# Threshold attention followed by a tanh-shrink layer, one core: one threshold shift for two tiles, earlier weights, DMA transposes from the second batch on, an earlier first projection and a last tile in halves

## The chip, the cores and the metric

One core of one Trainium2 chip. The time is the device time of one execution in microseconds (us). Stages are told from the profile of one execution; its span (first to last instruction) is some 2 us shorter than the device time.

## The reference, cut to what matters

```python
# q, k, v: (batch 8, heads 8, seq 576, head_dim 64), float32; tau = 0.02
scores = scale * q @ k.T
thresh = max(scores, axis=-1) - tau
scores = where(scores >= thresh, scores, -1e9)
attn   = softmax(scores)                      # over the surviving keys
x      = (attn @ v), heads side by side       # (4608, 512)
h = x @ w_in                                  # 512 -> 2048
g = h - tanh(h)
out = g @ w_out                               # 2048 -> 512
```

## The kernel before

Attention runs over 32 head pairs (four for each of eight batches), nine score tiles a pair: per head four whole tiles, which make two "duos" of an A and a B tile, and one M tile that both heads share. So 36 tiles are one batch. While batch m's attention runs, the hidden layer of batch m-1 and the projection of batch m-2 are slipped in as "layer steps" of four matmuls each. A last block holds the 64 remaining rows of every batch.

Names that the profile uses: `sc` the scaled scores with their row maximum `mx`; `nb` = tau - max, the shift; `z` = Prelu(sc + nb) with an enormous negative slope, so that a key below the threshold goes to a large negative number (`zm` where it is an M tile's); `zT` (or `psZ`, where TensorE does it) its transpose; `pT` = exp of it; `psO`, `osb`, `xT` the attention output on its way to the layers; `psH`, `th`, `g` the hidden layer; `psY`, `yo` the projection; `khl`, `qhl` the split of k and q on GpSimd, `kT`, `qT` their transposes, `kS` is kT with its two halves of 64 partitions exchanged; `wt` a piece of weights as loaded, `w_in_sb` and `w_out_sb` the cast weights.

Score and shift, per tile (VectorE):

```python
        mx = st_pool.tile([P, 1], F32, name="mx", tag="mx")
        nc.vector.tensor_scalar(
            out=sc, in0=ps[:, lo : lo + S], scalar1=SC, scalar2=None,
            op0=ALU.mult, op1=ALU.max, accum_out=mx,
        )
...
    def shift(i):
        sc, mx = scs[i]
        nb = st_pool.tile([P, 1], F32, name="nb", tag="nb")
        nc.vector.tensor_scalar(
            out=nb, in0=mx, scalar1=-1.0, scalar2=tau, op0=ALU.mult, op1=ALU.add
        )
```

The transpose of z, on TensorE for the first two batches (`NPE = 2 * HPAIR * TPP` tiles) and by DMA from batch 2 on:

```python
        if i < NPE:
            z = zts.pop(i)
            ps = ps_y.tile([P, 5 * P], BF16, name="psZ", tag="y")   # ps_y has one buffer
            for c in range(n):
                nc.tensor.matmul(..., rhs=ident_bf, is_transpose=True, ...)
            ...nc.scalar.activation(out=pt[...], in_=ps[:, 0 : n * P], func=ACT.Exp)
        # else: one exp over both tiles of the duo, from zT,
        # which kink() had made with nc.sync.dma_start_transpose(...)
```

kS and the weights (all of these DMAs are issued on the SyncE queue):

```python
            sw = qk_pool.tile([P, W], FP16, name="kS", tag="ks")
            nc.gpsimd.tensor_copy(out=sw[0:D, :], in_=m[D:P, :])
            nc.gpsimd.tensor_copy(out=sw[D:P, :], in_=m[0:D, :])
...
    wt_pool = pool("wt", 2)
    w_when = [4 * i + 3 for i in range(17)]
...
            if s + AHEAD in w_when:        # once per spacing: cast one, load the next
                if loaded:
                    w_cast()               # GpSimd
                piece = next(pieces, None)
                if piece:
                    w_load(piece)          # nc.sync.dma_start
```

`AHEAD = 7` and `MASK = 5` are leads in tiles: scores stand seven tiles, z five tiles ahead of the exp of the same tile.

Of the kernel before, what the change touches and what calls it, by code (L numbers as in the profile page):

```python
# [18 lines left out]
def kernel(  # L19
# [11 lines left out]
    nc = tc.nc  # L31
# [22 lines left out]
    NPE = 2 * HPAIR * TPP  # L54
# [4 lines left out]
    MASK = 5  # L59
# [21 lines left out]
    for i in range(NV):  # L81
        vb = const.tile([P, 2, 6, D + 1], BF16, name=f"vb{i}")
        nc.gpsimd.memset(vb[:, :, 4:6, :], 0.0)
        nc.vector.memset(vb[:, :, 0:4, D : D + 1], 1.0)
        nc.vector.memset(vb[0:64, :, 4, D : D + 1], 1.0)
        nc.vector.memset(vb[64:P, :, 5, D : D + 1], 1.0)
        vbs.append(vb)
# [3 lines left out]
    for i in range(NM):  # L91
# [9 lines left out]
    fold = const.tile([P, 64], BF16, name="fold")  # L101
    nc.vector.tensor_tensor(
        out=fold, in0=ident_bf[:, 0:64], in1=ident_bf[:, 64:P], op=ALU.add
    )

# [119 lines left out]
    def turn(p, t):  # L225
        hl = hls.pop((p, t))
        ps = ps_big.tile([P, W], FP16, name=f"ps_{t}", tag="big")
        for c in range(TPP):
            turn_chunk(
                ps[:, c * P : (c + 1) * P], c, hl[:, c, :, :].rearrange("p a d -> p (a d)")  # L230
            )
        m = qk_pool.tile([P, W], FP16, name=f"{t}T", tag=t)
        nc.vector.tensor_copy(out=m, in_=ps)  # L233
        mats[p, t] = m
        if t == "k":
            sw = qk_pool.tile([P, W], FP16, name="kS", tag="ks")
            nc.gpsimd.tensor_copy(out=sw[0:D, :], in_=m[D:P, :])  # L237
            nc.gpsimd.tensor_copy(out=sw[D:P, :], in_=m[0:D, :])  # L238
            mats[p, "ks"] = sw
# [25 lines left out]
    scs, zs, zts, pts, ops = {}, {}, {}, {}, {}  # L265
# [5 lines left out]
    def scores(i):  # L271
# [15 lines left out]
        else:  # L287
# [9 lines left out]
        mx = st_pool.tile([P, 1], F32, name="mx", tag="mx")  # L297
        nc.vector.tensor_scalar(  # L298
            out=sc, in0=ps[:, lo : lo + S], scalar1=SC, scalar2=None,
            op0=ALU.mult, op1=ALU.max, accum_out=mx,  # L300
        )
        scs[i] = sc, mx

    def shift(i):
        sc, mx = scs[i]
        nb = st_pool.tile([P, 1], F32, name="nb", tag="nb")
        nc.vector.tensor_scalar(  # L307
            out=nb, in0=mx, scalar1=-1.0, scalar2=tau, op0=ALU.mult, op1=ALU.add
        )
        scs[i] = sc, nb  # L310

    def kink(i):
        sc, nb = scs.pop(i)
# [20 lines left out]
    def weights(i):  # L334
# [4 lines left out]
        if i < NPE:  # L339
            z = zts.pop(i)  # L340
            ps = ps_y.tile([P, 5 * P], BF16, name="psZ", tag="y")
# [126 lines left out]
    def project(m, ms, part, ps, last):  # L468
        for n in range(4 * part, 4 * part + 4):
            nc.tensor.matmul(  # L470
                out=ps, lhsT=gs[m][:, n, ms * P : (ms + 1) * P],
                rhs=w_out_sb[:, n, :], start=(n == 0), stop=(n == DF_C - 1),
            )
        if part == 3:
            yo = y_pool.tile([P, d_model], F32, name="yo")
# [7 lines left out]
            else:  # L483
                for h in range(2):
                    b = 2 * ms + h
                    stores.append(
                        lambda b=b, h=h: nc.sync.dma_start(
                            out=out[b * S + MB : (b + 1) * S, :],
# [3 lines left out]

    def layers(m, tail):

        steps, cur = [], {}
# [8 lines left out]
        def y_step(ms, part):  # L504
            if part == 0:
                tag = ("y", "o")[ms % 2] if tail else "y"
                pl = {"y": ps_y, "o": ps_o}[tag]
                cur["y"] = pl.tile([P, d_model], F32, name="psY", tag=tag)
            project(m - 1, ms, part, cur["y"], tail and ms % 2)

        for a in range(16):
            if m < NMB:
                steps.append(lambda a=a: h_step(a))
            if m > 0:
                steps.append(lambda a=a: y_step(a // 4, a % 4))
        return steps

# [49 lines left out]
    for t in ("k", "q", "ks"):  # L567
        turn_first(t, 0)
    split_v(0)
# [3 lines left out]
    w_when = [4 * i + 3 for i in range(17)]  # L573
# [59 lines left out]
    while stage <= NMB:  # L633
# [45 lines left out]
```

## Time and profile before

| | before |
|---|---|
| device time, median of 4 runs | 551.97 us (551.58 to 552.21) |
| span of the profiled run | 549.4 us |
| TensorE / VectorE / ScalarE / GpSimd busy | 95 / 81 / 81 / 52 % |
| start and batch 0 (to the copy of its last pair's x) | 71.14 us |
| batch 1 | 58.25 us |
| batches 2 to 6 (59.16 or 59.17 each) | 295.82 us |
| batch 7 (no hidden layer of its own yet) | 50.86 us |
| tail, layers alone | 73.3 us |

The stage lengths are read from the trace: every fourth head pair's x copy closes a batch. The lines on which they rest stand in the prediction below. There and later, a line of waits says who waited, for whom, and then us in all, times and the longest; a line of the timeline gives start, length, engine, line and instruction, and in brackets the idle time before it and what ended that; L307 is line 307 of that run's own kernel, so the same instruction has another number in another kernel.

### The profile page before, as it was taken

Reading aid. Unit: us, or ns where it says so; the run is one execution under the profiler, and the core shown is the slowest. Engines: PE = TensorE matmul, PEld = TensorE weight load, DVE = VectorE, ACT = ScalarE, POOL = GpSimd, SP = SyncE. Lnnn points to the kernel's source line nnn. Section 1 sums busy time; section 2 is a strip of 40 time slices with the busy share of each in tenths; the row PEclk is TensorE's granted clock in tenths of the full one; section 3 lists DMA queues with packets and bytes.
Section 4 is the critical chain, followed back from the end, with each engine's and each line's share of the span. In section 5 each row is a group of like instructions: output and inputs, shape, how many; then the busy total and the mean of one; then the engine's idle time right before and its main releaser. Section 6 shows DMA issues by size and latency. Waiting matters only on the chain.

```text
span 549.4 us, 13518 instructions
## 1 busy us (share of the span) xinstructions
PE 521.8 (95%) x4954; PEld 302.4 (55%) x4954; DVE 444.1 (81%) x1349; ACT 443.3 (81%) x640; POOL 286.5 (52%) x372
## 2 busy tenths in 40 slices
PE   5888999999999999999999999999999999999996
PEld 2566666665555555555555555555555555444442
DVE  5888988898988999898889898898989888544430
ACT  3999999899899898989888988989898989533320
POOL 6788977666556666556555655666665620000000
PEclk9999999999999999999999999999999999999999
DMA  6755644437879888889977798877878966310103
GB/s 168 216 183 146 205 125 145 128 74 157 161 153 172 178 181 160 169 171 170 186 174 173 165 182 164 167 180 179 163 169 171 185 87 144 66 39 38 40 38 78
DMA packets 183011, 80.33 MB, mean 146 GB/s; under 512 B 150688, under 2 KB 175264, under 8 KB 182944
## 3 DMA queue, kind: packets, MB, share of 16 engines
q1 hardware_dynamic: 182512, 79.17, 65.0%
q8 instruction: 39, 0.64, 0.5%
q10 hardware_dynamic: 432, 0.30, 0.2%
q14 instruction: 28, 0.23, 0.2%
HBM read 37.75 MB, written 9.44 MB: 86 GB/s over the span
## 4 chain that ended last, share of the span: by engine, by line
PE 72%; DVE 16%; ACT 8%; issue 2%; DMA 1%; SPq 0%; ACTq 0%; DVEq 0%
PE psY L470 20%; PE psH L444 18%; PE psS L292 15%; DVE sc L298 6%; PE psO L389 5%; ACT pT L352 4%; PE psS L282 3%; ACT z L324 3%; DVE g L463 3%; PE psHt L444 3%; PE ps_q L221 2%; PE ps_k L221 2%; PE psZ L343 2%; DVE yo L479 1%; DVE kT L233 1%
## 5 line engine op out<-in xcount | busy, mean ns | idle before, releaser
L298 DVE TENSOR_SCALAR_CACHE_REDUCE sc<-psS 128x576 f32<-128x576 f32 x288 | 216.3, 751 | 19.8 <-PE psS L282 12.5
L324 ACT ACTIVATE z<-sc,nb 128x576 bf16<-128x576 f32 x256 | 195.7, 769 | 14.3 <-DVE nb L307 13.4
L470 PE MATMUL psY<-w_out_sb,g 128*128 128x512 bf16 x576 | 145.4, 379 | 0.0
L360 ACT ACTIVATE pT<-zT 128x1152 f16<-128x1152 bf16 (+1 forms) x120 | 127.8, 1065 | 0.0
L444 PE MATMUL psH<-xT,w_in_sb 128*128 128x512 bf16 x480 | 124.0, 379 | 0.3
L292 PE MATMUL psS<-kT,qT 128*128 128x512 f16 (+1 forms) x512 | 105.2, 287 | 10.1 <-DVE nb L307 7.6
L292 PEld LDWEIGHTS <-qT 128*128 128x128 f16 x1024 | 75.5, 98 | 68.1 <-issue 15.9
L237 POOL COPY kS<-kT 64x1152 f16<-64x1152 f16 x31 | 35.3, 1140 | 141.4 <-DVE nb L307 141.4
L463 DVE SCALAR_TENSOR_TENSOR g<-th,psH 128x512 bf16<-128x512 f32 x128 | 87.4, 683 | 22.0 <-ACT th L457 22.0
L292 PE MATMUL psS<-kS,qT 128*128 128x512 f16 x496 | 101.4, 286 | 0.0
L457 ACT ACTIVATE th<-psH 128x512 f32<-128x512 f32 x128 | 74.7, 584 | 17.8 <-PE psH L444 17.6
L470 PEld LDWEIGHTS <-g 128*128 128x128 bf16 x576 | 49.6, 98 | 57.7 <-issue 2.6
L444 PEld LDWEIGHTS <-w_in_sb 128*128 128x128 bf16 x576 | 49.3, 98 | 55.0 <-issue 2.7
L389 PEld LDWEIGHTS <-pT 128*128 128x128 f16 x1280 | 55.6, 98 | 24.3 <-ACT pT L360 2.1
L389 PE MATMUL psO<-vb,pT 128*128 128x65 bf16 x1280 | 61.2, 193 | 0.6 <-ACT pT L360 0.6
L352 ACT ACTIVATE pT<-psZ 128x640 f16<-128x640 bf16 (+1 forms) x72 | 47.2, 656 | 6.9 <-PE psZ L343 6.2
L307 DVE TENSOR_SCALAR nb<-mx 128x1 f32<-128x1 f32 x288 | 42.6, 148 | 3.4
L324 ACT ACTIVATE zm<-sc,nb 128x576 bf16<-128x576 f32 x32 | 24.8, 774 | 23.1 <-DVE nb L307 23.1
L183 POOL TENSOR_TENSOR qhl<-xs,qhl 128x576 f16<-128x576 f32 x31 | 39.7, 1280 | 2.6
L183 POOL TENSOR_TENSOR khl<-xs,khl 128x576 f16<-128x576 f32 x31 | 39.7, 1279 | 2.6
L238 POOL COPY kS<-kT 64x1152 f16<-64x1152 f16 x31 | 35.4, 1142 | 1.3
L343 PE MATMUL psZ<-ident_bf,z 128*128 128x128 bf16 x288 | 26.5, 219 | 4.5 <-ACT pT L352 4.3
(72 smaller groups left out, 561.6 us busy)
## 6 DMA issues: line engine op xcount, KB each, us to landing
vraw<-in_v_dram SPq DMA_DIRECT2D x32, 256.0 KB, 3.5
out_dram<-yo SPq DMA_DIRECT2D x32, 256.0 KB, 2.6
kraw<-in_k_dram SPq DMA_DIRECT2D x31, 256.0 KB, 3.1
qraw<-in_q_dram SPq DMA_DIRECT2D x31, 256.0 KB, 3.2
wt<-in_moe_w_in_dram SPq DMA_DIRECT2D x8, 512.0 KB, 4.4
wt<-in_moe_w_out_dram SPq DMA_DIRECT2D x8, 512.0 KB, 3.9
vraw<-in_v_dram SPq DMA_DIRECT2D x64, 32.0 KB, 2.9
zT<-z SPq DMA_TRANSPOSE x96, 3.3
```

The lines of the kernel that those rows point to most:

```text
L183: nc.gpsimd.tensor_tensor(out=hl[:, :, 1, :], in0=x, in1=hl[:, :, 0, :], op=ALU.subtract)
L292: nc.tensor.matmul(out=ps[:, dst], lhsT=lhs, rhs=kk[:, src], start=(n == 0), stop=(n == 1),)
L298: nc.vector.tensor_scalar(out=sc, in0=ps[:, lo : lo + S], scalar1=SC, scalar2=None, op0=ALU.mult, op1=ALU.max, accum_out=mx,)
L307: nc.vector.tensor_scalar(out=nb, in0=mx, scalar1=-1.0, scalar2=tau, op0=ALU.mult, op1=ALU.add)
L324: nc.scalar.activation(out=z, in_=sc, func=ACT.Prelu, bias=nb, scale=1.0, alpha=STEEP)
L352: nc.scalar.activation(out=pt[:, off * P : (off + n) * P], in_=ps[:, 0 : n * P], func=ACT.Exp)
L360: nc.scalar.activation(out=pt[:, 0 : n * P], in_=zts.pop(i)[:, 0:n, :], func=ACT.Exp)
L389: nc.tensor.matmul(out=po[:, (j - 1 - 5 * hh) + ab, :], lhsT=pt[:, blk * P : (blk + 1) * P], rhs=vb[:, hh, c, :], start=(n == 0), stop=(n ...
L444: nc.tensor.matmul(out=ps, lhsT=w_in_sb[:, c, n * P : (n + 1) * P], rhs=xs[m][:, c, :] if m < B else xR[:, c, :, :], start=(c == 0), stop= ...
L457: nc.scalar.activation(out=th, in_=ps, func=ACT.Tanh)
L463: nc.vector.scalar_tensor_tensor(out=gs[m][:, n, :], in0=th, scalar=-1.0, in1=ps, op0=ALU.mult, op1=ALU.add,)
L470: nc.tensor.matmul(out=ps, lhsT=gs[m][:, n, ms * P : (ms + 1) * P], rhs=w_out_sb[:, n, :], start=(n == 0), stop=(n == DF_C - 1),)
```

## The change

The intent is to take work off the engines at their limit. One shift serves both tiles of a duo; the lead of z falls from five tiles to four, so that both maxima of a duo exist in time. The DMA transposes (called the "crossbar" in places below) take over from batch 1 on instead of batch 2, counting from 0, and the batch that stays with TensorE alternates between two PSUM pools. kS comes by DMA for batch 0, weights come every three tiles instead of four, three projection steps move a stage earlier, and the last tile of the output is made and stored in halves.

```diff
-    NPE = 2 * HPAIR * TPP
+    NPE = HPAIR * TPP
-    MASK = 5
+    MASK = 4
...
-            nc.gpsimd.tensor_copy(out=sw[0:D, :], in_=m[D:P, :])
-            nc.gpsimd.tensor_copy(out=sw[D:P, :], in_=m[0:D, :])
+            for lo, hi in ((0, D), (D, 0)):
+                o, i = sw[lo : lo + D, :], m[hi : hi + D, :]
+                if p < HPAIR:
+                    nc.sync.dma_start(out=o, in_=i)
+                else:
+                    nc.gpsimd.tensor_copy(out=o, in_=i)
...
-        mx = st_pool.tile([P, 1], F32, name="mx", tag="mx")
+        if kind(j) == "B":
+            mx = mxs[i] = mxs.pop(i - 1)
+        else:
+            mx = mxs[i] = st_pool.tile([P, 2], F32, name="mx", tag="mx")
...
     def shift(i):
+        kd = kind(i % TPP)
+        if kd == "A":
+            return
+        n = 2 if kd == "B" else 1
+        nb = st_pool.tile([P, 2], F32, name="nb", tag="nb")
         nc.vector.tensor_scalar(
-            out=nb, in0=mx, scalar1=-1.0, scalar2=tau, op0=ALU.mult, op1=ALU.add
+            out=nb[:, 0:n], in0=mx[:, 0:n], scalar1=-1.0, scalar2=tau,
+            op0=ALU.mult, op1=ALU.add,
         )
...
-            ps = ps_y.tile([P, 5 * P], BF16, name="psZ", tag="y")
+            pl, tag = ((ps_y, "y"), (ps_h, "h"))[i % 2]
+            ps = pl.tile([P, 5 * P], BF16, name="psZ", tag=tag)
...
+    EARLY = 3        # projection steps of a block done in its own stage
+    # layers(): order of steps rebuilt for this; the last tile as two
+    # halves of 256 columns, one copied by ScalarE and stored on its queue
...
-    w_when = [4 * i + 3 for i in range(17)]
+    w_when = [3 * i + 2 for i in range(17)]
```

Left out: constants moved from VectorE to GpSimd or to later, and the bookkeeping of the layer steps.

More of the change, by code (lines that the diff above doesn't have):

```diff
@@ L83 @@
         nc.gpsimd.memset(vb[:, :, 4:6, :], 0.0)
-        nc.vector.memset(vb[:, :, 0:4, D : D + 1], 1.0)
-        nc.vector.memset(vb[0:64, :, 4, D : D + 1], 1.0)
-        nc.vector.memset(vb[64:P, :, 5, D : D + 1], 1.0)
+        nc.gpsimd.memset(vb[:, :, 0:4, D : D + 1], 1.0)
+        nc.gpsimd.memset(vb[0:64, :, 4, D : D + 1], 1.0)
+        nc.gpsimd.memset(vb[64:P, :, 5, D : D + 1], 1.0)
         vbs.append(vb)
@@ L100 @@
     nc.vector.memset(own[64:P, 1, :], 1.0)
-    fold = const.tile([P, 64], BF16, name="fold")
-    nc.vector.tensor_tensor(
-        out=fold, in0=ident_bf[:, 0:64], in1=ident_bf[:, 64:P], op=ALU.add
-    )
     pool = lambda name, bufs, **kw: ctx.enter_context(
@@ L264 @@
     REM = (slice(512, 576), slice(576, 640))
-    scs, zs, zts, pts, ops = {}, {}, {}, {}, {}
+    scs, mxs, nbs, zs, zts, pts, ops = {}, {}, {}, {}, {}, {}, {}
     def kind(j):
@@ L296, in scores @@
         sc = sc_pool.tile([P, S], F32, name="sc")
-        mx = st_pool.tile([P, 1], F32, name="mx", tag="mx")
+        if kind(j) == "B":
+            mx = mxs[i] = mxs.pop(i - 1)
+        else:
+            mx = mxs[i] = st_pool.tile([P, 2], F32, name="mx", tag="mx")
+        c = int(kind(j) == "B")
         nc.vector.tensor_scalar(
             out=sc, in0=ps[:, lo : lo + S], scalar1=SC, scalar2=None,
-            op0=ALU.mult, op1=ALU.max, accum_out=mx,
+            op0=ALU.mult, op1=ALU.max, accum_out=mx[:, c : c + 1],
         )
-        scs[i] = sc, mx
+        scs[i] = sc
     def shift(i):
-        sc, mx = scs[i]
-        nb = st_pool.tile([P, 1], F32, name="nb", tag="nb")
+        kd = kind(i % TPP)
+        if kd == "A":
+            return
+        n = 2 if kd == "B" else 1
+        mx = mxs.pop(i)
+        nb = st_pool.tile([P, 2], F32, name="nb", tag="nb")
         nc.vector.tensor_scalar(
-            out=nb, in0=mx, scalar1=-1.0, scalar2=tau, op0=ALU.mult, op1=ALU.add
-        )
-        scs[i] = sc, nb
+            out=nb[:, 0:n], in0=mx[:, 0:n], scalar1=-1.0, scalar2=tau,
+            op0=ALU.mult, op1=ALU.add,
+        )
+        nbs[i] = nb[:, n - 1 : n]
+        if kd == "B":
+            nbs[i - 1] = nb[:, 0:1]
     def kink(i):
-        sc, nb = scs.pop(i)
+        sc, nb = scs.pop(i), nbs.pop(i)
         kd = kind(i % TPP)
@@ L466, in shrink, with project @@
             )
-    def project(m, ms, part, ps, last):
+    def project(m, ms, part, ps, last, cols=slice(0, d_model)):
         for n in range(4 * part, 4 * part + 4):
@@ L471, in project @@
                 out=ps, lhsT=gs[m][:, n, ms * P : (ms + 1) * P],
-                rhs=w_out_sb[:, n, :], start=(n == 0), stop=(n == DF_C - 1),
+                rhs=w_out_sb[:, n, cols], start=(n == 0), stop=(n == DF_C - 1),
             )
         if part == 3:
-            yo = y_pool.tile([P, d_model], F32, name="yo")
+            nc_ = cols.stop - cols.start
+            yo = y_pool.tile([P, nc_], F32, name="yo")
             if last:
@@ L485, in project @@
                     b = 2 * ms + h
+                    eng = nc.scalar if h and nc_ < d_model else nc.sync
                     stores.append(
-                        lambda b=b, h=h: nc.sync.dma_start(
-                            out=out[b * S + MB : (b + 1) * S, :],
+                        lambda b=b, h=h, eng=eng: eng.dma_start(
+                            out=out[b * S + MB : (b + 1) * S, cols],
                             in_=yo[64 * h : 64 * h + 64, :],
@@ L491, in project @@
                     )
+    EARLY = 3
+    LAST = 1
+    quarters = lambda m: [(m, ms, part) for ms in range(4) for part in range(4)]
     def layers(m, tail):
-        steps, cur = [], {}
         def h_step(n):
@@ L502, in h_step, with y_step, y_half, ready @@
             hidden(m, n, ps)
-        def y_step(ms, part):
+        def y_step(m, ms, part):
             if part == 0:
-                tag = ("y", "o")[ms % 2] if tail else "y"
-                pl = {"y": ps_y, "o": ps_o}[tag]
-                cur["y"] = pl.tile([P, d_model], F32, name="psY", tag=tag)
-            project(m - 1, ms, part, cur["y"], tail and ms % 2)
-        for a in range(16):
-            if m < NMB:
-                steps.append(lambda a=a: h_step(a))
-            if m > 0:
-                steps.append(lambda a=a: y_step(a // 4, a % 4))
+                odd = ms % 2
+                pl, tag = (ps_o, "o") if tail and odd else (ps_y, "y")
+                ys[m, ms] = pl.tile([P, d_model], F32, name="psY", tag=tag), odd
+            ps, odd = ys[m, ms]
+            project(m, ms, part, ps, tail and odd)
+        def y_half(h):
+            n = d_model // 2
+            pl, tag = ((ps_y, "y"), (ps_o, "o"))[1 - h]
+            ps = pl.tile([P, n], F32, name="psY", tag=tag)
+            for part in range(4):
+                project(m, 3, part, ps, h == 0, slice(h * n, h * n + n))
+        now = quarters(m - 1)[EARLY:] if m > 0 else []
+        if m < NMB - 1:
+            now += quarters(m)[:EARLY]
+        else:
+            now += quarters(m)[:12]
+        n = 16 + len(now)
+        ahead = n - max(0, EARLY - 3) - LAST if m < NMB - 1 else n - 9 - LAST
+        steps, at, i = [], [], 0
+        def ready(y):
+            last = 4 * y[2] + 3
+            return y[0] < m or len(at) > last and at[last] + 2 < i
+        while now or len(at) < 16:
+            if len(at) < 16 and (
+                not now or not ready(now[0]) or len(at) * ahead <= i * 16
+            ):
+                steps.append(lambda a=len(at): h_step(a))
+                at.append(i)
+            elif ready(now[0]):
+                steps.append(lambda y=now.pop(0): y_step(*y))
+            else:
+                steps.append(lambda: None)
+            i += 1
+        if m == NMB - 1:
+            steps += [lambda h=h: y_half(h) for h in range(2)]
         return steps
+    ys = {}
     def w_pieces():
@@ L568 @@
         turn_first(t, 0)
+    fold = const.tile([P, 64], BF16, name="fold")
+    nc.vector.tensor_tensor(
+        out=fold, in0=ident_bf[:, 0:64], in1=ident_bf[:, 64:P], op=ALU.add
+    )
     split_v(0)
@@ L631 @@
                     w_load(piece)
-    while stage <= NMB:
+    while stage < NMB:
         for step in layers(stage, True):
```

## The prediction

> **What bounds the kernel now.** I read four views in this order: the span cut into stages, who waited for whom in each stage, the chain of work that ended last, and the timeline where a stage showed idle TensorE. The stages are the 36 tiles of one batch each, cut where the last head pair's x is copied out (every ninth tile).
>
> ```profile
> core 0: us, PE busy (x) PEld busy (x) DVE busy (x) ACT busy (x) POOL busy (x), PEclk, DMA share, GB/s
> 23.00:71.14 48.14, 42.97 (x597) 31.35 (x597) 42.60 (x143) 45.50 (x73) 43.22 (x54) 1.00 0.57 174
> 71.14:129.39 58.25, 54.67 (x647) 36.12 (x646) 50.98 (x161) 53.16 (x87) 42.32 (x53) 1.00 0.43 119
> ...
> 188.56:247.72 59.16, 58.23 (x561) 33.46 (x560) 53.30 (x165) 52.75 (x73) 34.46 (x45) 1.00 0.85 171
> ...
> 476.07:549.40 73.33, 68.72 (x319) 30.92 (x316) 26.03 (x40) 22.63 (x38) 0.00 (x0) 0.99 0.14 44
> ```
>
> The first row is most of batch 0 (attention alone), the second batch 1 (attention plus the first layer of batch 0), the third one of five alike batches (attention plus both layers), the last the layers left when attention is over. Batch 0 is ScalarE's: 45.50 of 48.14 us. Batch 1 is near ScalarE's limit (53.16 of 58.25). The alike batches and the tail are TensorE's (58.23 of 59.16; 68.72 of 73.33). So one instruction has a different worth in each stage. Who waits, for ScalarE in batch 0, then in batch 1:
>
> ```profile
> ACT pT L352 <- PE psZ L343: 2.2, 8, 0.5
> ```
> ```profile
> ACT pT L352 <- PE psZ L343: 3.2, 8, 0.6
> ACT zm L324 <- DVE nb L307: 0.9, 2, 0.5
> ACT z L324 <- DVE nb L307: 0.7, 1, 0.7
> ```
>
> In batch 0 ScalarE waits for nothing but the TensorE transposes; in batch 1 3.2 of its 4.8 us of waits are those. In an alike batch TensorE's idle time lies at the batch's end, in the four tiles that carry no layer step:
>
> ```profile
> 241.73 0.69 DVE L479 COPY yo<-psY 128x512 f32<-128x512 f32 x1
> 241.84 0.67 PE L221 MATMUL ps_q<-ident_f,qhl 128*128 128x128 f16 x9
> 242.59 0.41 PE L292 MATMUL psS<-kS,qT 128*128 128x512 f16 x2
> 242.93 0.75 DVE L233 COPY qT<-ps_q 128x1152 f16<-128x1152 f16 x1
> 243.74 0.41 PE L292 MATMUL psS<-kT,qT 128*128 128x512 f16 x2 [0.74 <-DVE nb L307]
> ```
>
> The scores at 243.74 wait for the PSUM buffer that the qT copy empties at 243.68. A pair of score matmuls takes 0.245 us from start to start, so they come 0.90 us late (242.59 to 243.74). Further on in the same gap of tiles I count 0.31, 0.16, 0.08 and 0.10 in the same way: 1.55 us a batch. The chain ends with
>
> ```profile
> 530.11 14.69 PE psY L470 x68
> ```
>
> TensorE without a pause: 14.69 / 68 = 0.216 us each, so a layer step (four matmuls of 512 columns) is 0.864 us.
>
> [...] a 128x1 nb takes 148 ns, a 128x576 sc 751. [...] the last row's stores (128 KB each) take 2.2 to 2.4 us to land, so halving bytes saves little and issuing side by side saves more. [...]
>
> **The change, part by part.**
>
> *Start.* The fold add (0.18 us) and twelve small memsets (about 0.1 each) leave VectorE ahead of the first kT copy, which started at 6.97 though its transposes ended at 6.67. The first z started at 13.50. I give 0.2.
>
> *Batch 0.* It keeps its TensorE transposes, but they alternate between two PSUM pools, so the next tile's transposes need not wait for ScalarE to read this one's. The waits of 2.2 us should nearly vanish; the other instructions stay. ScalarE's floor is 48.14 - 2.2 = 45.9; I take 46.25: 1.9 gained. The shared nb takes 16 of 36 nb from VectorE (each of 16 duos does one instead of two, four M tiles keep theirs), some 0.12 each: worthless here, since VectorE has 42.6 of 48.1. kS by DMA takes 2.3 us a pair from GpSimd and the faster weight casts give some back: no engine at its limit moves.
>
> *Batch 1.* Its 36 tiles go from TensorE to DMA transposes. TensorE loses 164 transposes of about 0.056 us (9.2 us) and gains three projection steps (2.6 us), so it is no longer near its limit. ScalarE's exps become 16 of 1150 ns and 4 of 720 in place of 20 of 705 and 16 of 597: 21.3 against 23.7 us, 2.4 less, of which part is pipelining overlap. The same ScalarE load stands in the alike batch, 52.75 busy; with 0.4 of short gaps its floor is 53.2. To that come the nb waits (1.3, a bit less than 1.6 now) and, new, waits for transposes: exp comes four tiles after z and not five. A transpose takes 3.3 us from issue to landing, four tiles are about 6 us, but the queue is also busy with loads; I put 1.0. Sum 55.5, gain 2.75. That is the bound, not TensorE (about 47 us): the three early projection steps are free.
>
> *Alike batches, five ends with the gap described.* TensorE's work does not change: three steps come in, three go out. What changes is VectorE in the gap. The last yo copy of a stage moves six tiles earlier (0.69 us out of the crowded stretch), and three nb go. The qT copy is then held by its own transposes (end 242.51) and not by VectorE, so it starts about 0.4 earlier; in the four tiles after it two nb less give 0.24. So 0.65 of the 1.55 a gap, 5 x 0.65 = 3.25.
>
> *Last attention tiles.* One tile less of lead puts the last z behind the exp before it; its transpose still lands in time (its exp at 472.83 came 1.3 us after landing). I count 0.1 lost.
>
> *Tail.* Three steps fewer: 80 to 77, 3 x 0.864 = 2.59. The remainder block's projection now follows its own hidden layer at once: the quarter that needs the last g comes 1.73 us after that layer's start where g needs 2.38 (0.63 + 0.69 after a 1.06 us run-up), but only its fourth matmul reads that g, 0.65 later; loading its weights ahead may cost 0.25. Last tile: now the last matmul ends at 544.79, copy to 545.46, stores issued at 545.5 and 546.0, landed at 547.75 and 548.36. With a half tile the copy is about 0.38 instead of 0.59 and the two stores leave two queues together: 0.2 + 0.6 = 0.8. Sum 2.59 - 0.25 + 0.8 = 3.15.
>
> Total: 0.2 + 1.9 + 2.75 + 3.25 - 0.1 + 3.15 = 11.15, so 551.78 - 11.15 = 540.6; I say 540.5.
>
> **Rivals.** (a) *The transpose wait takes the place of the psZ wait.* For it: in the alike batches exp starts a median of 4.0 us after its transpose landed (my reading of landing times against exp starts) and sometimes 1 to 1.7; one tile (1.5) less leaves some below zero, and DMA share will be above 0.85 in batch 1, as the same transposes run in a shorter time. Against: no ScalarE wait for a DMA is listed now. If each of batch 1's 20 exps waited 0.3 more, batch 1 would gain nothing much: 543 to 544. In the alike batches such waits would not matter, as ScalarE has some 6 us to spare there. (b) *VectorE was the true limit in the gap and all of it goes.* Then five gaps give 1.55 each, 7.75 in place of 3.25, and the time is 536. For it: VectorE is busy without a break from 237.3 to 247.8. Against: after the qT copy it still has four sc, a norm and the x copy, work that the change leaves. (c) *The gains on VectorE, GpSimd and TensorE transposes are all off the path*, and only the tail counts: 548.5. Against: in batches 0 and 1 the psZ waits stand on the bounding engine.
>
> **Range and chances.** Batch 1 is open by 2 us either way, the gaps by +4 or -2, batch 0 and the tail by 0.6 each; taken as independent about 3 us, so 536.5 to 544.5. The 2% mark is 540.74, at my centre; the gaps have more room upward than down. Faster by over 2%: 0.54; within: 0.45; slower: 0.01.
>
> **What would show it.** In the profile after: batch 0 shorter by about 2 us with the psZ waits near zero; batch 1 near 55.5 with TensorE clearly idle and ScalarE over 94% busy; the alike batches near 58.5 from 59.16; 77 steps' worth in the tail, and about 3.8 us in place of 4.6 after the last matmul. I am wrong if ScalarE shows long waits for zT's transposes, if the alike batches stay at 59.16 (then nb and yo were not what held the qT copy), or if they fall to 57.6.

What is left of the paragraph with the cuts is measured in the trace of before; for its remark that halving bytes saves little the trace has loads of k of 32 KB that land a median of 2.8 us after issue and of 256 KB that take 3.1. That issuing side by side saves more was an estimate from the two last stores, issued at 545.5 and 546.0. The 0.056 us of a transpose can be read from it too: nine ps_q transposes take 0.67 us where one takes 0.22. The overlap on ScalarE is there as well: in batch 1 its groups add up to 61.6 us, and it is busy for 53.16. The 0.12 of a shared nb, the 0.25 for loading weights ahead and the 0.38 of a half-tile copy were estimates.

## More of the kernel before

In the view of groups by shape, a line gives engine, operation, output and input with their shapes, the count, then busy us and the mean ns of one, then idle time before:

```profile
L307 DVE TENSOR_SCALAR nb<-mx 128x1 f32<-128x1 f32 x288 | 42.6, 148 | 3.4
```

The 288 shifts take 148 ns each, and the shortest and longest of them lie within 140 and 156 ns. It looks like an operation with a constant price.

## The result, and the profile after

The changed kernel's median is **558.27 us** (556.97 to 558.72, 4 runs) against 551.97: a ratio of 1.0111, with a 95% interval from 1.0092 to 1.0130. That is within 2%, on the slower side, and outside of the predicted range. Ratios here and below are the mean time of one kernel's fast runs over the mean of the other's fast runs of the same rounds, so not quite the ratio of the quoted medians.

The same cuts as before, the stage table of the kernel after (columns as in its header line: stage, its length, busy time of each engine, granted clock, DMA share):

```profile
core 0: us, PE busy (x) PEld busy (x) DVE busy (x) ACT busy (x) POOL busy (x), PEclk, DMA share, GB/s
24.22:77.16 52.94, 42.12 (x545) 30.01 (x543) 42.12 (x122) 42.26 (x68) 41.91 (x53) 0.94 0.74 207
77.16:134.87 57.71, 49.08 (x510) 29.03 (x509) 53.25 (x146) 52.01 (x72) 39.04 (x50) 1.00 0.89 175
...
195.24:254.62 59.38, 58.62 (x561) 33.62 (x560) 53.80 (x149) 52.44 (x73) 34.46 (x45) 1.00 0.84 172
484.96:555.20 70.24, 66.24 (x323) 31.20 (x320) 26.42 (x41) 22.43 (x38) 0.00 (x0) 1.00 0.14 46
```

| stage | before | predicted change | after | change |
|---|---|---|---|---|
| start and batch 0 | 71.14 | -2.1 | 77.16 | **+6.0** |
| batch 1 | 58.25 | -2.75 | 57.71 | -0.5 |
| batches 2 to 6 | 295.82 | -3.25 | 298.18 | **+2.4** |
| batch 7 | 50.86 | +0.1 | 51.91 | +1.0 |
| tail | 73.3 | -3.15 | 70.2 | -3.1 |
| span | 549.4 | -11.15 | 555.2 | +5.8 |

The tail came as foreseen. Start and batch 0 lost 8 us against the prediction, the alike batches 5.6, batch 1 2.2. In the alike batch VectorE has 16 instructions fewer (149 for 165) and yet more busy time (53.80 for 53.30). One group tells why, by shape as above:

```profile
L316 DVE TENSOR_SCALAR nb<-mx 128x2 f32<-128x2 f32 x128 | 38.3, 299 | 0.8
L316 DVE TENSOR_SCALAR nb<-mx 128x1 f32<-128x1 f32 x32 | 4.6, 144 | 0.0
```

The 128 shared shifts take 299 ns on average, twice the price of the narrow ones, so that 160 instructions cost what 288 did: 42.9 us for 42.6. The answer for that one line gives the spread (shortest, median and longest in ns):

```profile
L316 DVE TENSOR_SCALAR nb<-mx x160: 137/164/1286, 11.9 to 475.1; 128x2 f32<-128x2 f32 x128, 128x1 f32<-128x1 f32 x32
```

A median of 164 with a longest of 1286 isn't a price, it is a wait inside of the instruction. The timeline (start, length, engine, instruction) of the kernel after shows one:

```profile
89.70 1.28 POOL L179 TENSOR_TENSOR khl<-xs,khl 128x576 f16<-128x576 f32 x1
89.71 1.29 DVE L316 TENSOR_SCALAR nb<-mx 128x2 f32<-128x2 f32 x1
...
90.91 0.74 DVE L302 TENSOR_SCALAR_CACHE_REDUCE sc<-psS 128x576 f32<-128x576 f32 x1
90.94 0.67 POOL L175 TENSOR_SCALAR xs<-qraw 128x576 f32<-128x576 f32 x1
```

The shift begins 0.01 us after a GpSimd instruction and ends with it; VectorE starts nothing else until 90.91. (The score instruction that follows then lies beside another GpSimd instruction and takes its usual 0.74 us.) The same meeting in the kernel before is harmless:

```profile
230.16 1.28 POOL L183 TENSOR_TENSOR khl<-xs,khl 128x576 f16<-128x576 f32 x1
...
231.22 0.14 DVE L307 TENSOR_SCALAR nb<-mx 128x1 f32<-128x1 f32 x1
```

I went through all 160 shifts of the trace after: 58 lasted over 0.2 us, and every one of them ended 22 to 29 ns after the end of a GpSimd instruction that overlapped it. Their excess over 150 ns adds up to 18.3 us of VectorE's time. The expectations below call this wait a lock, and I keep the word; it stands for what was measured here and for nothing behind it. The narrow form is the control: in the trace before, 139 of the 288 shifts began and ended inside of a GpSimd instruction, and none took over 156 ns; of the 128 wide ones after, none lay inside of one. (In a_ks, below, one of 128 did, with 158 ns; the GpSimd instruction had begun 11 ns before it.)

The second loss lies in batch 0. Who waited for whom there (us in all, times, longest), kernel after:

```profile
ACT pT L365 <- PE psZ L356: 8.8, 8, 4.4
POOL w_in_sb L584 <- DMA wt<-in_moe_w_in_dram: 8.8, 2, 4.9
...
PE ps_k L217 <- POOL khl L179: 7.4, 3, 3.6
DVE kT L229 <- PE ps_k L217: 6.8, 3, 3.8
```

ScalarE's psZ waits, 2.2 us before and predicted to vanish, are 8.8, and behind them stands a ring: GpSimd waits for a weight piece, TensorE for GpSimd's split of k, the kT copy for TensorE. The timeline of the kernel after, with SPq the DMA queue:

```profile
27.44 0.76 DVE L229 COPY kT<-ps_k 128x1152 f16<-128x1152 f16 x1 [1.71 <-PE ps_k L217]
...
28.26 1.16 SPq L236 DMA_DIRECT2D kS<-kT  x2
...
32.34 1.01 SPq L596 DMA_DIRECT2D wt<-in_moe_w_in_dram  x2
...
36.48 1.04 POOL L584 CAST w_in_sb<-wt 128x1024 bf16<-128x1024 f32 x1 [3.87 <-DMA wt<-in_moe_w_in_dram]
...
38.98 1.27 POOL L179 TENSOR_TENSOR khl<-xs,khl 128x576 f16<-128x576 f32 x1
```

GpSimd sits 3.87 us idle at the weight cast, and the split of the next pair's k (at 38.98) stands behind that cast in its order. Its k had been there for long: it was issued at 20.84 and 21.27, and the slowest load of k in this trace took 6.2 us to land. kS, issued on the same queue, goes only when kT is there: the queue waited 2.7 us for it before 28.26, and the weight piece was issued after that, at 32.34.

The 0.94 under PEclk comes from two stretches of 3.41 us, from 27.27 and from 54.58 us, in which the granted clock was 0.50; nine ps_k transposes took 1.14 us at 54.94, and 0.68 at 26.73. In the 3.41 us before each, TensorE had been busy for only 1.27 and 0.13 us; its waits for those splits of k were 2.13 and 3.64 us. That the one brings the other is not shown, as no run varies it. TensorE worked for 3.41 and 3.05 us in the two stretches, so as an estimate from these figures at most half of that, 3.2 us, is lost to the clock; no run separates it from the waits.

### The profile page after: what moved, and what is told of

Same layout as the page of the kernel before. It is cut to its first block, busy times and chain, and to the rows that moved or that the text cites. A ratio compares the mean times of both kernels' runs of the same rounds, so it can differ in the third digit from the quotient of the medians.

```text
span 555.2 us, 13146 instructions
## 1 busy us (share of the span) xinstructions
PE 517.2 (93%) x4806; PEld 296.8 (53%) x4806; DVE 450.5 (81%) x1210; ACT 439.5 (79%) x624; POOL 280.6 (51%) x378
## 4 chain that ended last, share of the span: by engine, by line
PE 68%; DVE 14%; issue 6%; DMA 4%; POOL 4%; ACT 3%; SPq 1%; POOLq 0%; ACTq 0%; DVEq 0%
PE psY L483 20%; PE psH L457 16%; PE psS L292 15%; PE psO L402 5%; DVE sc L302 4%; DVE g L476 3%; PE psHt L457 2%; PE psS L282 2%; PE ps_q L217 2%; DMA zT<-z 2%; PE ps_k L217 2%; DVE nb L316 2%; DVE yo L493 2%; DVE qT L229 1%; PE psO L391 1%
## 5 line engine op out<-in xcount | busy, mean ns | idle before, releaser
L336 ACT ACTIVATE z<-sc,nb 128x576 bf16<-128x576 f32 x256 | 192.4, 767 | 26.4 <-DVE nb L316 26.1
L373 ACT ACTIVATE pT<-zT 128x1152 f16<-128x1152 bf16 (+1 forms) x140 | 149.4, 1067 | 6.5 <-DMA zT<-z 4.8
L483 PE MATMUL psY<-w_out_sb,g 128*128 128x512 bf16 (+1 forms) x592 | 146.0, 374 | 0.0
L238 POOL COPY kS<-kT 64x1152 f16<-64x1152 f16 x56 | 63.9, 1141 | 142.3 <-DVE nb L316 141.0
L402 PE MATMUL psO<-vb,pT 128*128 128x65 bf16 x1280 | 61.6, 194 | 0.6 <-ACT pT L373 0.6
L316 DVE TENSOR_SCALAR nb<-mx 128x2 f32<-128x2 f32 (+1 forms) x160 | 42.9, 268 | 0.8
L217 PE MATMUL ps_k<-ident_f,khl 128*128 128x128 f16 x288 | 22.2, 223 | 13.9 <-POOL khl L179 7.4
L229 DVE COPY qT<-ps_q 128x1152 f16<-128x1152 f16 x31 | 23.5, 757 | 11.0 <-PE ps_q L217 10.9
L365 ACT ACTIVATE pT<-psZ 128x640 f16<-128x640 bf16 (+1 forms) x36 | 23.6, 655 | 10.4 <-PE psZ L356 10.3
L493 DVE COPY yo<-psY 128x512 f32<-128x512 f32 (+1 forms) x31 | 21.1, 680 | 10.7 <-PE psY L483 6.7
```

The lines of the kernel that those rows point to most:

```text
L238: nc.gpsimd.tensor_copy(out=o, in_=i)
L316: nc.vector.tensor_scalar(out=nb[:, 0:n], in0=mx[:, 0:n], scalar1=-1.0, scalar2=tau, op0=ALU.mult, op1=ALU.add,)
L336: nc.scalar.activation(out=z, in_=sc, func=ACT.Prelu, bias=nb, scale=1.0, alpha=STEEP)
L373: nc.scalar.activation(out=pt[:, 0 : n * P], in_=zts.pop(i)[:, 0:n, :], func=ACT.Exp)
L402: nc.tensor.matmul(out=po[:, (j - 1 - 5 * hh) + ab, :], lhsT=pt[:, blk * P : (blk + 1) * P], rhs=vb[:, hh, c, :], start=(n == 0), stop=(n ...
L483: nc.tensor.matmul(out=ps, lhsT=gs[m][:, n, ms * P : (ms + 1) * P], rhs=w_out_sb[:, n, cols], start=(n == 0), stop=(n == DF_C - 1),)
```

## The experiments

Each group of kernels ran beside its own runs of the kernel before on the same chip, so ratios are compared and not medians across groups; a per cent of the kernel before is 5.5 us. Unless said otherwise results are correct, the time is the median of four runs, and "before" there had a median between 551.59 and 552.11. One run of the kernel before was slow (610.91 us, clock 0.853) and is left out. "Against after" means the difference of the two ratios to before.

### Undo one part at a time

**a_nb1**: the kernel after with a narrow shift per tile, all else kept.

```diff
+        for c in range(n):
             nc.vector.tensor_scalar(
-                out=nb[:, 0:n], in0=mx[:, 0:n], ...
+                out=nb[:, c : c + 1], in0=mx[:, c : c + 1], ...
```

> The changed kernel, with the shared 128x2 threshold shift taken back to one 128x1 shift per tile (same place in the order). Theory L (lock): the 128x2 form waits for a running GpSimd instruction to end, 17.7 us over all; without it no nb above 0.2 us, alike batches fall from 59.4 to 58.6-58.8, batch 1 from 57.7 to about 55.5, batch 0 little (1.7 us of nb waits there, GpSimd itself is late): total about 550 to 553 from 558.3. Rival S (size): 128x2 is merely a longer instruction and VectorE was not what delayed TensorE: within 1 us of 558.3.

Measured: 553.26 us, ratio 1.0027 (1.0010 to 1.0043): 4.6 us less than after. The 288 shifts are back at 145 ns (longest 156), batches 3 to 6 at 59.07 to 59.08 each, where after had 59.38 to 59.61 and before 59.16. So the shared shift costs, although it saves 128 instructions. The total is just above the range expected of theory L, and two of its figures missed: batch 1 did not fall to 55.5 but took 58.26, and the alike batches did not reach 58.8. The gain lies in batches 2 to 6 (2.5 us in all) and in the three pairs of batch 0 after the first x (38.82 for 40.95), where little was expected.

**a_ks**: the kernel after with kS by GpSimd for every pair.

```diff
-                if p < HPAIR:
+                if p < 0:
                     nc.sync.dma_start(out=o, in_=i)
```

> The changed kernel, with kS of the first pairs copied by GpSimd again instead of by DMA. Theory Q (queue): the kS transfer waits in the one DMA queue for kT, the weight pieces behind it land late, GpSimd waits for them in its order (15.7 us) and splits k late, which TensorE waits for (7.4 us); without it these waits go and batch 0 falls from 53 (batch of x to x) to about 48, total about 552 to 553. Rival W: the denser weight loading alone fills the queue and GpSimd, whoever makes kS: the waits stay and the total stays within 1.5 us of 558, or rises since GpSimd gets 2.3 us a pair more.

Measured: 552.60 us, ratio 1.0016 (0.9999 to 1.0033): 5.2 us less than after. GpSimd's waits for w_in are gone from batch 0, and batch 0's three pairs after the first x went from 40.95 to 36.78 us. Batch 1, however, grew from 57.71 to 60.05: part of the loss only moved on.

**a_w4**: the kernel after with the old spacing of the weights.

```diff
-    w_when = [3 * i + 2 for i in range(17)]
+    w_when = [4 * i + 3 for i in range(17)]
```

> The changed kernel, with the weight pieces loaded every 4 tiles again instead of every 3, kS still by DMA. Theory Q: the kS transfer still blocks the queue, but a piece has 4 tiles to land: GpSimd's waits for weights shrink but are not gone; total 553 to 556. Rival W (density alone is the cause): GpSimd's waits for weights and TensorE's for khl both go, total about 552.

Measured: 553.59 us, ratio 1.0026 (1.0010 to 1.0042): 4.7 us less than after. The three pairs of batch 0 take 36.12, though GpSimd still waits for weights: 9.4 us for w_in, all in the start and batch 0 (the longest, 5.1, stands before the split of a q and not of a k), and 5.4 for w_out later; batch 1 takes 60.33. So either of the two, kS off the queue or weights further apart, brings batch 0 back to what it was before the change (36.15). The ring needs both.

**a_nb1_ks**: the first two together.

```diff
 # a_nb1's loop and a_ks's condition in one kernel
```

> The changed kernel with both suspects undone: one 128x1 shift per tile, kS by GpSimd. If the two losses are separate they add: 558.3 - 5.0 - 5.7 = 547.6, batch 0 about 36.5, alike batches 59.07, tail 70.2. Batch 1 is open: about 58.3 as without the shared shift alone, or 60 as with kS alone; if one loss hid behind the other the total is 549 to 552.

Measured: 549.03 us, ratio 0.9958 (0.9937 to 0.9978). The two undoings give 8.4 us together where they gave 4.6 and 5.2 alone, 1.4 us short of the sum. With intervals of about 1 us on each ratio this can't be told from full addition, and by the expectation 549 lies at the border of the two theories; so the losses are separate in the main, and a part of one may hide behind the other.

### The shift by itself, in the kernel before

**b_nb2**: the kernel before with the shared shift and the lead of four that it needs.

```diff
-    MASK = 5
+    MASK = 4
 # and mx, nb as [P, 2], one tensor_scalar per duo, as in the change
```

> The kernel before, with nothing but the shared 128x2 shift (and the lead of four tiles that it needs). Theory L: 128x2 shifts last up to 1.3 us where GpSimd runs, TensorE's waits in the alike batches grow from 2.5 to about 3, total 552.5 to 556, a loss. Rival S: half the nb instructions on VectorE and nothing else, 0 to 3 us gained: 549 to 552.

Measured: 558.58 us, ratio 1.0118 (1.0100 to 1.0136): +6.5 us, more than the whole change. The 160 shifts take 47.3 us, longest 1275 ns; every alike batch takes 60.16 to 60.19 for 59.16. The loss is larger than theory L expected.

**b_mask4**: the kernel before with the shorter lead and nothing else.

```diff
-    MASK = 5
+    MASK = 4
```

> Control: the kernel before with the lead of four tiles alone, one shift per tile. Theory L puts the whole loss of the shared shift on the lock: this run within 1 us of the kernel before (552 to 553). If the lead is what cost: about 558, as with the shared shift.

Measured: 551.35 us, ratio 0.9995 (0.9980 to 1.0010); every stage after the first x within 0.03 us of before. In that kernel the lead is free, so the 6.5 us of b_nb2 are the shared shift's.

**b_wide**: the kernel before with 288 shifts, none shared, each merely two elements wide (the second element is a preset column that nobody uses).

```diff
+    mxs = [const.tile([P, 2], F32, name=f"mx{i}") for i in range(12)]   # preset to 0
-        nb = st_pool.tile([P, 1], F32, name="nb", tag="nb")
+        nb = st_pool.tile([P, 2], F32, name="nb", tag="nb")
...
-        scs[i] = sc, nb
+        scs[i] = sc, nb[:, 0:1]
```

> The kernel before with each of its 288 shifts made 128x2 (the second column is not used), nothing merged. Theory L (a 128x2 shift cannot start while a GpSimd instruction runs): 2.25 times as many exposed instructions as the merged form, many at 0.3 to 1.3 us, total nb time 70 to 90 us and the kernel 8 to 18 us slower (560 to 570). Rival S (only the count and the size of instructions matter): one more element each, 552 plus or minus 0.5.

Measured: 572.21 us, ratio 1.0372 (1.0354 to 1.0390): +20.5 us. The group by shape:

```profile
L313 DVE TENSOR_SCALAR nb<-mx 128x2 f32<-128x2 f32 x288 | 92.0, 319 | 3.4
```

Nothing was merged or moved here; apart from twelve presets of 60 ns at the very start the order of the instructions is that of before, and one element more per partition makes 148 ns into 319 (the total is 2 us above the range expected). In this trace 130 of the 288 lasted over 0.2 us, again each with its end 21 to 27 ns after a GpSimd instruction's, and none of the 288 lay inside of one. That settles it: the width costs, not the sharing. Why two elements wait and one does not, no run shows, and other widths of the shift were not run. Not every wider instruction waits: the 128x576 score instruction kept its usual 0.74 us beside GpSimd in the timeline shown above, and all 288 of them in the trace before lie between 741 and 760 ns.

### The kS queue, the lead and the weights

**a_m5_ks**: the kernel after with lead five, a narrow shift per tile and kS by GpSimd.

```diff
-    MASK = 4
+    MASK = 5
 # mx, nb and kS as in the kernel before
```

> The same, and the lead of the exponent's input back to five tiles (which one shift per tile allows). Theory T (transpose latency): batch 1 is long because z, the crossbar transpose and the exp, four tiles apart, hold up ScalarE and through it the score buffers; with five tiles ScalarE's waits for zT nearly vanish and batch 1 falls from about 58 to 55-56.5, total 1.5 to 3 us under the run with four. Rival V: VectorE and its coupling to TensorE hold batch 1; no change within 0.5 us.

Measured: 546.07 us, ratio 0.9902 (0.9887 to 0.9917): 3.1 us less than a_nb1_ks, which differs by the lead and the layout of mx. Stage by stage the gain lies in the start (0.6), batch 1 (58.85 to 57.98) and batch 2 (59.70 to 59.06); batches 3 to 6 are within 0.1. The total is as theory T expected, but batch 1 is not: it lost 0.9 us and not the 1.5 or more foreseen. So the shorter lead, free in the kernel before, is not free here. That it costs where DMA transposes meet the loading of weights is a guess: the weights have landed by 79 us, and batch 2 gains without them.

**a_m5_ks_w4**: the same with the weights every four tiles.

```diff
-    w_when = [3 * i + 2 for i in range(17)]
+    w_when = [4 * i + 3 for i in range(17)]
```

> The same, with the weight pieces every 4 tiles as before. If the denser weight loading still costs (queue, GpSimd) once kS is off the queue: 0.5 to 2 us faster than with 3 tiles. If it is free: within 0.5 us; if w_out then comes too late for the early projection steps: slower, with TensorE waiting for w_out.

Measured: 545.31 us, ratio 0.9890 (0.9862 to 0.9918), not to be told from a_m5_ks. But the time moved: batch 0 fell from 36.32 to 33.38 us (fewer weights fall into it), and batch 1 rose from 57.98 to 59.73. Its stage row, then two of its waits:

```profile
66.22:125.95 59.73, 49.09 (x502) 28.84 (x510) 51.09 (x161) 53.05 (x73) 43.31 (x54) 1.00 1.00 212
```
```profile
POOL w_out_sb L572 <- DMA wt<-in_moe_w_out_dram: 9.8, 3, 5.5
...
ACT pT L361 <- DMA zT<-z: 4.7, 4, 1.7
```

The DMA engines are busy all of batch 1 (share 1.00), and both GpSimd and ScalarE wait for transfers.

**a_now**: the same kernel: the w_out pieces are cast from a constant tile and never loaded. Its output is wrong, which doesn't matter for the time. It shows what batch 1 costs without that traffic, the casts kept.

```diff
+        if width == d_model:
+            loaded.append((flat, stand_in, i, cols))
+            return
```

> Wrong result on purpose: the run that was 545.3, with w_out's pieces cast by GpSimd from a resident tile and not fetched (4.2 MB less to move, mostly in batch 1, whose DMA share was 1.00). If batch 1 (59.7) is held by full DMA engines: it falls to 55.5-57 with DMA share 0.85-0.9, total 541.5 to 543.5. If ScalarE, VectorE or TensorE hold it: within 1 us of 59.7.

Measured: 539.74 us, ratio 0.9784 (0.9769 to 0.9800). Its batch 1:

```profile
66.50:121.06 54.56, 49.06 (x511) 29.03 (x510) 50.83 (x162) 51.73 (x73) 43.22 (x54) 1.00 0.84 172
```

With every engine's work the same, 5.2 us of batch 1 were the loading of w_out, GpSimd's waiting for it included. That is somewhat more than was expected.

**a_npe2**: a_m5_ks_w4 with batch 1's transposes back on TensorE.

```diff
-    NPE = HPAIR * TPP
+    NPE = 2 * HPAIR * TPP
-    EARLY = 3
+    EARLY = 0
```

(The early projection had to go with it: it holds the PSUM buffer that those transposes need. So the crossbar in batch 1 is what makes the early projection possible.)

> The run that was 545.3 with the crossbar only from batch 3, and so without projection steps in their own block's stage (they and TensorE's transposes want the same PSUM buffer); one shift per tile, two PSUM pools for the transposes. If crossbar plus early steps are worth their 2.6 us in the tail: 547.5 to 548.5. If the crossbar's load on the DMA engines costs batch 1 as much as the tail gains: batch 1 about 56-57 in place of 59.7, total 544.5 to 546.

Measured: 548.85 us, ratio 0.9948 (0.9933 to 0.9963). Batch 1 takes 61.03 us with a DMA share of only 0.41 and TensorE busy 55.53; ScalarE waits 4.8 us for psZ. So against this run the crossbar in batch 1 is worth 1.3 us there even with the weights in its way. The 54.56 without them is 6.5 us less, but TensorE's transposes were not run without the weights. And the kernel before, whose transposes in batch 1 are TensorE's too, but through one PSUM pool, takes only 58.25 there; why a_npe2 takes 2.8 us more was not looked for. The tail is cleaner: by the same cuts it takes 72.8 us here, 73.3 before and 70.1 in a_m5_ks_w4, so the half tiles and the new order of the last block gave 0.5 and the three early steps 2.6, as the prediction had them (0.8 - 0.25 and 2.59).

**a_wbuf**: a_m5_ks with eight weight buffers in place of two: a load every two tiles from the start, so that no weight is loaded in batch 1, and a cast every three and a half tiles, apart from the loads.

```diff
-    wt_pool = pool("wt", 2)
+    wt_pool = pool("wt", 8)
-    w_when = [3 * i + 2 for i in range(17)]
+    load_when = [2 * i + 2 for i in range(16)]
+    cast_when = [7 * i // 2 + 6 for i in range(16)]
```

> The run that was 546.1 (one shift per tile, lead five, kS by GpSimd), with eight weight buffers in place of two: weights fetched every 2 tiles, in batch 0, and cast every 3.5 tiles. If full DMA engines hold batch 1: batch 1 falls from 58.0 to 55-56.5 with DMA share near 0.85, batch 0 stays near 36.3 or less; total 541.5 to 544. If not: 545 to 547.

Measured: 541.71 us, ratio 0.9810 (0.9793 to 0.9827), correct. The stages:

```profile
33.15:68.61 35.46, 30.82 (x426) 21.90 (x424) 31.91 (x109) 33.40 (x53) 33.68 (x42) 1.00 0.67 201
68.61:123.11 54.50, 49.03 (x511) 28.99 (x510) 50.83 (x161) 51.66 (x73) 41.78 (x53) 1.00 0.83 171
123.11:182.16 59.05, 58.23 (x561) 33.46 (x560) 53.61 (x165) 52.72 (x73) 34.46 (x44) 1.00 0.84 168
```

Batch 1 is where a_now had it, at 54.50, with right results.

**a_wbuf_kdma**: the same with kS by DMA for batch 0.

```diff
-                if p < 0:
+                if p < HPAIR:
```

> The same with kS by DMA in batch 0. If kS by DMA is harmful only through weight pieces that GpSimd awaits right behind it: no long GpSimd waits for weights now, and with 2.3 us a pair less on GpSimd batch 0 is equal or up to 2 us shorter: total within 2 us under the run without. If waiting for kT in the queue delays the loads of q, k and v by itself: batch 0 longer by 2 us or more.

Measured: 545.55 us, ratio 0.9879 (0.9861 to 0.9897). The first x comes at 38.83 us for 33.15, the rest of batch 0 takes 33.26 for 35.46. Its waits up to the first x:

```profile
POOL w_in_sb L572 <- DMA wt<-in_moe_w_in_dram: 8.1, 1, 8.1
```

One single wait of 8.1 us, in the start; later pairs gain. Neither branch of the expectation came as written: the total is 3.8 us longer, yet batch 0 after the first x is 2.2 shorter. So kS by DMA isn't bad in itself: in these runs it was bad where a load that somebody waits for stands behind it.

### Does a longer lead help? (failed)

**a_m6_ks**: a_m5_ks with z six tiles ahead.

```diff
-    MASK = 5
+    MASK = 6
-    z_pool = pool("z", 4)
-    zt_pool = pool("zt", 4)
+    z_pool = pool("z", 5)
+    zt_pool = pool("zt", 5)
```

> Lead of six tiles instead of five (a buffer more for z and zT), otherwise the run that was 546.1. If the transposes' latency still holds batch 1: batch 1 falls from 58.0 to 56-57, total 544.5 to 545.5. If bandwidth of the DMA engines or VectorE holds it: batch 1 within 0.3, total within 0.5 of 546.1. The alike batches do not move.

Measured: 604.12 us, ratio 1.0949 (1.0931 to 1.0967). z now follows scores by one tile only, and ScalarE waits for a shift that VectorE has just been given:

```profile
ACT z L324 <- DVE nb L307: 59.5, 99, 1.6
ACT zm L324 <- DVE nb L307: 27.9, 30, 3.7
```

**a_m6b_ks**: the same with one more score buffer, in case that it was the buffers.

```diff
-    sc_pool = pool("sc", AHEAD - MASK + 2)
+    sc_pool = pool("sc", AHEAD - MASK + 3)
```

> Lead of six tiles with four score buffers, otherwise the run that was 546.1. If the last six-tile run was slow for its three score buffers: the alike batches are back at 59.1. If latency of a transpose holds batch 1: 56-57 in place of 58.0, total 544.5 to 545.5; if the DMA engines' load does: within 0.6 of 58.0, total 545.5 to 546.7.

Measured: 606.62 us, ratio 1.1001 (1.0958 to 1.1044), with the same waits (59.7 and 28.0 us). It was not the buffers. Whether more lead would hide late transposes in batch 1 is not answered by these two, since what they add at the other end is larger; it would need scores eight tiles ahead.

### The version that the experiments point to

**a_best**: a_wbuf with kS by DMA only for the last two pairs of batch 0.

```diff
-                if p < 0:
+                if 1 < p < HPAIR:
```

> The run that was 545.6 (eight weight buffers, one shift per tile, lead five, kS by DMA in batch 0), with kS of pair 1 by GpSimd. If the loss was the queue waiting for the first kT in the start alone: first x back to about 33.2, batch 0 between 33.3 and 34, total 539.5 to 541. If kS by DMA costs wherever it stands in front of weights: first x or batch 0 1.5 us or more longer than that, total 541.5 or more.

Measured: 540.90 us (540.47 to 542.16, 5 runs), ratio 0.9798 (0.9783 to 0.9813) to before, correct. That is 11.1 us under the kernel before and 17 under the changed one. Its advantage over a_wbuf (0.9810, 0.9793 to 0.9827, another group) is within the error of both. Its span of 539.1 us lies at 67.17 for start and batch 0, 54.92 for batch 1, 295.28 for batches 2 to 6, 51.50 for batch 7 and 70.3 for the tail.

## Why the prediction was wrong

By its own steps, with the size of each miss in spans:

1. **The shared shift** (failed). The steps "The shared nb takes 16 of 36 nb from VectorE ..., some 0.12 each" and "in the four tiles after it two nb less give 0.24" held the price of an instruction to be its count times a fixed cost. For that it had only the two prices of the trace of before, 148 ns for a 128x1 nb and 751 for a 128x576 sc. But the two elements that remained in the instruction made it wait for GpSimd (up to 1286 ns in the kernel after), where the one-element form took 156 ns at most (before, a_nb1). Shown: the width alone costs 20.5 us (b_wide); the shared form costs 6.5 us in the kernel before (b_nb2) and its undoing gives back 4.6 in the kernel after (a_nb1). The ends of all 58 long shifts in the kernel after, 22 to 29 ns after a GpSimd instruction's, show what they waited for; what in the chip makes them wait was not shown.

2. **kS by DMA and faster weights** (failed). The step was "kS by DMA takes 2.3 us a pair from GpSimd and the faster weight casts give some back: no engine at its limit moves". I weighed engines' work and left out the order in the queue: kS waits for kT (2.7 us of the queue), the weights issued behind it come late, GpSimd's list stops at their cast (3.87 us), and the next k is split late, from which kT and kS come. Shown: taking away either half of it, a_ks or a_w4, brings batch 0 after its first x from 40.95 to 36.8 or 36.1 us (36.15 before). Start and batch 0 were to gain 2.1 and lost 6.0, 1.2 of it before the first x.

3. **Batch 1** (half right). 55.5 was predicted, 57.71 measured. The reading of ScalarE as the bound was good (52.0 busy, where 94% of the stage was foreseen and 90% came) and the figure is undercut, at 54.5 to 54.9, whenever weights are not loaded in this batch (a_now, a_wbuf, a_best). The terms that were mis-sized are ScalarE's waits: in the kernel after it waits 3.2 us for nb, where I put 1.3, and 1.5 for zT, where I put 1.0. Undoing the shared shift only exchanged them (2.3 and 2.1, and 58.26 in all, in a_nb1). Rival (a), transposes too late, is part of it: with more of the weights in this batch ScalarE waits 4.7 us for zT (a_m5_ks_w4), without them 0.3 at most (a_now, a_wbuf, a_best). A high DMA share as such is not the cause, for a_best has 0.88 in this batch and takes 54.92, and the kernel after 0.89 and 57.71; it is the weight transfers. Whether by their bytes, by their place in the queue before the transposes, or through GpSimd, which waits for them (9.8 us in a_m5_ks_w4), no run separates. The sum for TensorE was off too, without effect: 54.67 - 9.2 + 2.6 is 48.1 and not "about 47", and 49.1 came.

4. **Alike batches** (mechanism right, sum wrong). -0.65 each was predicted. The stall of the qT copy did fall as foreseen: the timeline of the kernel after in the crowded gap has the score matmuls 0.52 us late in place of 0.90 (from 250.13 to 250.90, less the 0.245 of a pair):

```profile
250.09 0.76 DVE L229 COPY qT<-ps_q 128x1152 f16<-128x1152 f16 x1 [0.31 <-PE ps_q L217]
250.13 0.41 PE L292 MATMUL psS<-kS,qT 128*128 128x512 f16 x2
...
250.90 0.41 PE L292 MATMUL psS<-kT,qT 128*128 128x512 f16 x2 [0.36 <-DVE qT L229]
```

   But the yo copy that left the gap came to stand before a g elsewhere in the batch, and TensorE waits for that g, 0.32 us here:

```profile
224.68 0.69 DVE L493 COPY yo<-psY 128x512 f32<-128x512 f32 x1
...
225.28 0.68 DVE L476 SCALAR_TENSOR_TENSOR g<-th,psH 128x512 bf16<-128x512 f32 x1
...
226.01 1.02 PE L457 MATMUL psH<-xT,w_in_sb 128*128 128x512 bf16 x4 [0.32 <-DVE g L476]
```

   It is so without the lock too. TensorE's waits in one alike batch, first of the kernel before, then of a_nb1 (us in all, times, longest):

```profile
PE psS L292 <- DVE nb L307: 0.7, 1, 0.7
```
```profile
PE psS L292 <- DVE nb L317: 0.4, 1, 0.4
PE psH L458 <- DVE g L477: 0.3, 1, 0.3
```

   What one wait lost, the other took. So batches without the lock stand at 59.05 to 59.08 (a_m5_ks, a_nb1) for 59.16: 0.1 gained and not 0.65; a_npe2, without the early steps, has 59.16 and the wait of before. With the lock, 0.2 to 0.45 a batch are lost from batch 3 on. Batch 2 alone lost 1.2 (60.37); undoing the shared shift (59.38) or kS by DMA (59.47) takes most of that off, and why was not looked for. The step that failed is that work moved out of a crowded stretch was counted as gone.

5. **Batch 0's double transposes** (right as far as seen, and undersized). Predicted 1.9 and 0.2 for the start; without the two losses (a_m5_ks_w4) start and batch 0 take 66.22, 4.9 less than before: 2.1 before the first x and 2.8 after it. No ScalarE wait for psZ is left in its batch 0, as predicted; no run undid the second pool alone. That term helped to bring the repaired kernel's total, -10.3 us of span, near the -11.15 of the prediction; the agreement is one of sums, not of terms.

6. **Last attention batch.** "I count 0.1 lost" was 1.0 with the lock and 0.6 without. a_npe2, without the early projection steps, takes 50.87 as before, so the 0.6 comes with those steps; how was not looked for.

7. **Tail** (right). -3.15 predicted, -3.1 measured: 77 steps, half-tile copies of 0.37 and 0.42 us against the 0.38 assumed. From the end of the last matmul it took 4.0 us, for 3.8 foreseen and 4.6 before. The difference is a wait that I had not seen: the last copy stood 3 us for one of two output buffers, as the group says, while its matmuls were in part still running:

```profile
L493 DVE COPY yo<-psY 128x256 f32<-128x256 f32 x1 | 0.4, 424 | 3.0 <-DMA out_dram<-yo 3.0
```

   The estimate for the stores rests on the 2.2 to 2.4 us that the last row's took in the trace of before (128 KB each); the 64 KB stores of the half tiles took 2.0 us on SyncE's queue and 2.2 on ScalarE's (medians).

## What to carry to other kernels

Before you merge small VectorE instructions, ask which form the merged one takes: two elements a partition in place of one made an operation that took at most 156 ns beside GpSimd wait for it, 319 ns on average and 20.5 us of kernel time in b_wide, so look at the spread of durations in a group and not at its mean alone. Before you hand a copy to a DMA queue, ask what stands behind it in that queue, and who waits for that with other work behind it: GpSimd sat idle for 3.87 us at once in the kernel after and for 8.1 in a_wbuf_kdma. Work that is moved within a stage isn't removed: name the instruction that it now precedes.
